# An attention and gated-layer kernel: two small matrix products written as halves of 64 columns

## The chip, the cores and the metric

The kernel runs on one NeuronCore of a Trainium2 chip. The metric is the device time of one execution in microseconds (us); lower is better. The time before is the median of three runs.

## What is computed

The reference is attention with random features, followed by a gated layer. q, k and v have 8 batches, 8 heads, 576 positions and 64 columns. With x scaled by 1 / 64^(1/4):

```
phi(x) = exp(h - max(h)) / sqrt(128),   h = x @ omega.T - sum(x*x)/2      # 128 features
kv  = phi(k).T @ v        z   = sum over positions of phi(k)
num = phi(q) @ kv         den = phi(q) @ z + 1e-6
x   = num / den           # heads side by side: 4608 x 512
out = (sigmoid(x @ w_gate) * (x @ w_val)) @ w_out     # 512 -> 1536 -> 512
```

All arrays are f32.

## The kernel before

**Attention.** Two batches make a unit u (four units), two heads a pair p (four pairs). The 2 x 576 positions of a unit are nine tiles of 128; tile 4, the middle one (`MID`), holds 64 positions of either batch b. Everything below runs for each u, p and b.

Keys (`keys`, from line 809): a projection of three matmuls per tile (`projected`, lines 774 to 776), the maximum on DVE, the exponential on ACT (line 841, tiles `kp` and, for the middle tile, `kmid`). Then comes the keys group at line 865: for each of the two heads, five products that accumulate over five tiles into `pkv`, 128 features by 66 columns (64 of v, and ones for z). The stationary operand is 128 x 128, the exponentials of a tile; the moving one is v, 128 x 66. Both are plain f32, and each product of the program leaves two matmul records and two weight loads in the profile. There are 32 keys groups of 10 products, so 640 records. ACT copies the result to `kv` (line 875).

Queries (`queries`, from line 882): projection, maximum, a subtraction on DVE (`h`, line 898), a transpose on PE (line 912, tile `pt`), the exponential on ACT (`qp`, line 917), and then line 933: query features by `kv` into `pn`, 128 x 66 for each tile and head. DVE divides by the last column (lines 944 to 950, first step `den`), PE transposes the result (line 958), ACT copies it and SP stores it to `xT` in DRAM. Query groups hold two tiles (four products, 64 such groups) or the middle tile alone (16 groups). In a middle group the 64 positions of either batch need another `kv`, so each product is already written as two of 64 columns, one for each half of the output's partitions.

**Gated layer.** While attention runs, the first part of the gated layer uses what attention has stored: chunks of `xT` are read back, split in a high and a low part on ACT and POOL (`xe`), and multiplied with the first four weight tiles (line 444, tile `gv`, 960 matmuls). Weights for the rest are converted on DVE and POOL at the same time. Behind attention come the remaining `gv` products, then the second pass (line 557, `gw`) and the output products (line 670, `po`).

**What sets the order.** The first phase has a planner of its own: `Turns`, with coroutines for each piece of work. A piece asks for an engine with a rank; `turn` also waits for free buffers; `use` books the estimated cost in ns on that engine. Whoever is ready and has the lowest rank goes next, and the instructions are written in that order. The `gv` products have the last rank (`2 * FILL`), so the planner puts them where PE would otherwise be free. Before chunk 0 has arrived, four matmuls into a bank that nobody reads (`unread`, line 780) are written behind each projection. The estimate for a keys group is `2 * (MID + 1) * 112` ns, for a query group of n products `n * 112`.

Of the kernel before, what the change touches and what calls it, by code (L numbers as in the profile page):

```python
# [20 lines left out]
P = 128  # L21
# [2 lines left out]
NP = H // 2  # L24
MID = T // 2


GROUPS = {"k": (((0, 1), (2, 3), (4,)), ((5, 6), (7, 8))), "q": (((0, 1), (2, 3)), ((4,), (5, 6), (7, 8)))}
E = D + 2
# [30 lines left out]
class Turns:  # L60
# [45 lines left out]
    def use(self, e, t, cost, lag):  # L106
        self.free[e] = t + cost
        return t + cost + lag
# [63 lines left out]
def attn_glu_kernel(ctx: ExitStack, tc, qT, kT, qn, kn, va, om, ident, w, out):  # L172
    nc = tc.nc
# [21 lines left out]
    def bank(i, name):  # L195
        return ps.tile([P, 512], F32, tag=f"bank{i}", bufs=1, name=name)
# [14 lines left out]
    use = turns.use  # L211
# [20 lines left out]
    def turn(engine, t, *shelves, rank=None):  # L232

        while True:
            t = yield engine, t, rank
            ready = t
            for s in shelves:
                place = s.next() if isinstance(s, Ring) else min(s.places, default=None)
                if place is None:
                    yield s  # L240
                    break
                ready = max(ready, place[0])
            else:
                if ready <= t:
                    return t, [s.take() for s in shelves]
            t = max(ready, turns.now)

    def after(event, t):
        while event.left:
            yield event  # L250
        return max(t, event.time)

    def act(n, pointer=False):
        return (165 if pointer else 120) + 0.833 * n

    def dve(n):
        return (n + 140) / 0.96
# [7 lines left out]
    PE_LAG, LAG, ISSUE, LANDS = 260, 100, 420, 3200  # L265
# [447 lines left out]
    def spot(pool, tag, i, shape, name, dtype=F32):  # L713
        return pool.tile(shape, dtype, tag=f"{tag}{i}", bufs=1, name=name)
# [84 lines left out]
    def source(pool, name, u, p, b, src):  # L799
        t0, t1 = span(name, b)  # L800
        n = (t1 - t0) * P
        held = ("raw", "v") if name == "k" else ("raw",)
        at, taken = yield from turn("SP", 0, *(places[h] for h in held))
        raw = spot(pool, "raw", taken[0], [P, (MID + 1) * P], f"raw{name}{u}_{p}_{b}")
        nc.sync.dma_start(out=raw[:, :n], in_=src[u, p, :, t0 * P : t1 * P])
        at = use("SP", at, ISSUE, LANDS)
        return at, raw, t0, taken

    def released(event, name, i):
        t = yield from after(event, 0)  # L810
        places[name].put(i, t)

    def keys(pool, u, p, b):
        rank = order["k", u, p, b]
        at, raw, t0, (i, vi) = yield from source(pool, "k", u, p, b, kT)
        v = spot(pool, "v", vi, [P, MID + 1, 2, E], f"v{u}_{p}_{b}")
        av = yield "SP", 0, rank + 0.5
        nc.sync.dma_start(out=v, in_=va[u, p, b])
        av = use("SP", av, ISSUE, LANDS)
        last = Event(turns, len(GROUPS["k"][b]))  # L820
        turns.start(released(last, "raw", i), rank)
        kp, held = {}, []
        every = kexp_ready[u, p, b]
        k_begun[u, p, b].set(at)

        def group(tiles):
            at_, id_, pp, hm, s, place, own = yield from projected(pool, "k", u, p, b, raw, t0, tiles, at, last)
            nt = len(tiles)
            at_ = yield "DVE", at_, None
            nb = pool.tile([P, 2, 2], F32, tag="nb", bufs=12, name=f"nb{id_}")[:, :nt]  # L830
            nc.vector.scalar_tensor_tensor(  # L831
                out=nb, in0=s, scalar=-1.0, in1=hm, op0=ALU.mult, op1=ALU.subtract
            )
            at_ = use("DVE", at_, 160, LAG)
            tag = "kmid" if tiles[0] == MID else "kp"
            at_, (k,) = yield from turn("ACT", at_, places[tag])
            x = spot(pool, tag, k, [P, 2 * nt, M], f"{tag}{id_}")
            for i, t in enumerate(tiles):
                kp[t] = x[:, 2 * i : 2 * i + 2, :]
                for h in range(2):  # L840
                    nc.scalar.activation(  # L841
                        out=kp[t][:, h, :], in_=pp[:, 2 * i + h, :], func=AF.Exp,
                        bias=nb[:, i, h : h + 1], scale=SCALE,
                    )
            at_ = use("ACT", at_, 2 * nt * act(M, True), LAG)
            if tag == "kmid":
                kmid[u, p] = kp[MID], k
            else:
                held.append((tag, k))
            banks.put(place, at_)  # L850
            pps.put(own, at_)
            every.set(at_)

        for tiles in GROUPS["k"][b]:
            turns.start(group(tiles), rank)
        at = yield from after(every, av)
        if b:
            at = yield from after(kexp_ready[u, p, 0], at)
            kp[MID], mid = kmid.pop((u, p))
            held.append(("kmid", mid))  # L860
        at, (place, k) = yield from turn("PE", at, banks, places["kv"])
        pkv = bank(place, f"pkv{u}_{p}_{b}")[:, : 2 * E].rearrange("p (h e) -> p h e", h=2)
        for h in range(2):
            for i in range(MID + 1):
                nc.tensor.matmul(  # L865
                    pkv[:, h, :], lhsT=kp[b * MID + i][:, h, :], rhs=v[:, i, h, :],
                    start=(i == 0), stop=(i == MID),
                )
        at = use("PE", at, 2 * (MID + 1) * 112, PE_LAG)
        places["v"].put(vi, at)  # L870
        for tag, i in held:
            places[tag].put(i, at)
        at = yield "ACT", at, None
        kv = spot(pool, "kv", k, [P, 2, E], f"kv{u}_{p}_{b}")
        nc.scalar.activation(out=kv, in_=pkv, func=AF.Copy)
        at = use("ACT", at, act(2 * E), LAG)
        banks.put(place, at)
        kvs[u, p, b] = kv
        kv_ready[u, p, b].set(at)
        turns.start(released(kv_users[u, p, b], "kv", k), rank)  # L880

    def queries(pool, u, p, b):
# [6 lines left out]
        def group(tiles):  # L889
            at_ = yield from after(kexp_ready[u, p, b], start)  # L890
            at_, id_, pp, hm, s, place, own = yield from projected(pool, "q", u, p, b, raw, t0, tiles, at_, last)
            nt = len(tiles)
            n = 2 * nt
# [12 lines left out]
            at_ = use("DVE", at_, 240 + dve(n * M), LAG)  # L906
# [6 lines left out]
            at_ = use("PE", at_, n * 109, PE_LAG)  # L913
            places["h"].put(hi, at_)
            at_ = yield "ACT", at_, None
            qp = spot(pool, "qp", qi, [P, 4, P], f"qp{id_}")[:, :n]
            nc.scalar.activation(out=qp, in_=pt, func=AF.Exp)  # L917
            at_ = use("ACT", at_, act(n * P), LAG)
            banks.put(place, at_)
            mid = tiles[0] == MID  # L920
            at_ = yield from after(kv_ready[u, p, b], at_)
            if mid:
                at_ = yield from after(kv_ready[u, p, 0], at_)
            at_, (place, xi) = yield from turn("PE", at_, banks, places["x"])
            pn = bank(place, f"pn{id_}")[:, : n * E].rearrange("p (i e) -> p i e", e=E)
            for i, t in enumerate(tiles):
                if t == MID:
                    mine = ((0, slice(0, P // 2)), (1, slice(P // 2, P)))
                else:
                    mine = ((b, slice(0, P)),)  # L930
                for h in range(2):
                    for bb, r in mine:
                        nc.tensor.matmul(  # L933
                            pn[r, 2 * i + h, :], lhsT=qp[:, 2 * i + h, r], rhs=kvs[u, p, bb][:, h, :],
                            start=True, stop=True,
                        )
            at_ = use("PE", at_, n * 112, PE_LAG)
            places["qp"].put(qi, at_)
            kv_users[u, p, b].set(at_)
            if mid:  # L940
# [1 line left out]
            at_ = yield "DVE", at_, None  # L942
# [10 lines left out]
            at_ = use("DVE", at_, 440 + dve(n * D), LAG)  # L953
# [9 lines left out]
            at_ = use("PE", at_, nt * 109, PE_LAG)  # L963
            places["x"].put(xi, at_)
            at_ = yield "ACT", at_, None
            xs = spot(pool, "xs", si, [P, 2 * P], f"xs{id_}")[:, : nt * P]
            nc.scalar.activation(out=xs, in_=px, func=AF.Copy)
            at_ = use("ACT", at_, act(nt * P), LAG)
            banks.put(place, at_)
            at_ = yield "SP", at_, -1  # L970
            o = u * 2 * S + tiles[0] * P
            nc.sync.dma_start(out=xT[p, :, o : o + nt * P], in_=xs)
            at_ = use("SP", at_, ISSUE, LANDS)
# [5 lines left out]
        for tiles in GROUPS["q"][b]:  # L979
            turns.start(group(tiles), rank)  # L980
# [157 lines left out]
```

## Time and profile before

| | us |
|---|---|
| median of three runs | 1275.88 (1274.79 to 1282.54) |
| the profiled execution | 1282.16 |
| its span, first to last instruction | 1280.1 |
| PE busy | 1185.1 (93%) |
| DVE busy | 891.5 (70%) |
| POOL, ACT busy | 565.7, 530.8 |
| line 865, matmul records, busy up to 560 us | 91.1 |
| line 933, matmul records, busy up to 560 us | 75.5 |

PE is TensorE's matmuls, PEld its weight loads, DVE VectorE, ACT ScalarE, POOL GpSimd, SP the engine that issues most transfers. A row of the timeline gives the start and the length of a run of like instructions, in us from the span's start. Records overlap: a matmul's record is longer than the step to the next one, so a cost is read from starts and not from the length of one record. The granted clock is the share of TensorE's full clock; its mean over the profiled execution is 0.949.

### The profile page before, as it was taken

The numbers are of one execution on the slowest core, as the hardware profiler recorded it, in microseconds if no ns is written. First come the engines' busy times: TensorE is split into PE (matmuls) and PEld (weight loads), VectorE is DVE, ScalarE is ACT, GpSimd is POOL, SyncE is SP. The second block draws the span as 40 slices with busy tenths as digits, with TensorE's granted clock in tenths as the row PEclk, the third lists the DMA queues.
The fourth block names the chain that finished last, engine by engine and source line by source line (L and its number), as shares of the span: only waits on it lengthen the run. The fifth ranks groups of instructions, "written<-read, shape, count | busy, mean of one in ns | idle before, by whom it ended". The sixth has DMA issues, their size and how long they took to land.

```text
span 1280.1 us, 24128 instructions
## 1 busy us (share of the span) xinstructions
PE 1185.1 (93%) x8936; PEld 1133.7 (89%) x8936; DVE 891.5 (70%) x1885; ACT 530.8 (41%) x1168; POOL 565.7 (44%) x591
## 2 busy tenths in 40 slices
PE   4859999899989898966999999999999799999998
PEld 4859989798978787855899999999999799999998
DVE  5885787779887988752475566655667777777665
ACT  4536464546453655423332223322234333433332
POOL 2544263525373545254176666666666411111111
PEclk7886998899989898978999999999999999999999
DMA  6636366546764665345423332333328575666653
GB/s 233 217 122 190 93 195 227 178 149 210 244 216 167 219 245 184 106 134 219 170 87 120 120 120 103 132 120 120 121 89 288 188 208 187 201 193 196 194 186 110
DMA packets 107734, 217.59 MB, mean 170 GB/s; under 512 B 10848, under 2 KB 48992, under 8 KB 105312
## 3 DMA queue, kind: packets, MB, share of 16 engines
q1 hardware_dynamic: 102288, 206.54, 48.0%
q10 hardware_dynamic: 5328, 9.51, 2.0%
q8 instruction: 70, 1.15, 0.4%
q14 instruction: 48, 0.39, 0.1%
HBM read 141.82 MB, written 74.19 MB: 169 GB/s over the span
## 4 chain that ended last, share of the span: by engine, by line
PE 75%; DVE 7%; DMA 6%; issue 6%; POOL 4%; SPq 1%; ACT 1%; DVEq 0%; POOLq 0%; ACTq 0%
PE gw L557 26%; PE po L670 20%; PE gv L444 10%; PE pkv L865 5%; PE pnq L933 4%; PE ptq L912 2%; PE ppq L774 1%; PE ppk L774 1%; PE ppk L776 1%; PE ppk L775 1%; PE ppq L775 1%; PE ppq L776 1%; DMA ye<-ye 1%; DVE nbk L831 1%; POOL xe L417 1%
## 5 line engine op out<-in xcount | busy, mean ns | idle before, releaser
L557 PE MATMUL gw<-xl,u 128*128 128x256 f32 x3024 | 363.5, 283 | 6.3 <-DVE u L537 3.7
L557 PEld LDWEIGHTS gw<-xl,u 128*128 128x128 f32 x3024 | 362.3, 190 | 7.5 <-DVE u L537 4.5
L670 PE MATMUL po<-u,yh 128*128 128x256 f32 x1512 | 272.5, 283 | 0.0
L670 PEld LDWEIGHTS po<-u,yh 128*128 128x128 f32 x1512 | 234.6, 190 | 0.0
L670 PE MATMUL po<-u,yl 128*128 128x256 f32 x756 | 214.0, 283 | 5.5 <-POOL yl L146 4.1
L444 PE MATMUL gv<-xe,wh 128*128 128x512 f32 (+1 forms) x640 | 198.8, 386 | 10.2 <-POOL xe L417 10.2
L145 ACT ACTIVATE yh<-yr 128x896 fp32r<-128x896 f32 x108 | 99.0, 948 | 166.7 <-DMA yr<-yl 56.3
L670 PEld LDWEIGHTS po<-u,yl 128*128 128x128 f32 x756 | 144.2, 191 | 6.2 <-POOL yl L146 4.3
L444 PEld LDWEIGHTS gv<-xe,wh 128*128 128x128 f32 x640 | 117.7, 195 | 29.8 <-POOL xe L417 14.0
L444 PE MATMUL gv<-xe,wl 128*128 128x512 f32 (+1 forms) x320 | 124.6, 389 | 18.2 <-ACT xe L407 18.2
L146 POOL TENSOR_TENSOR yl<-yr,yh 128x896 fp32r<-128x896 f32 x18 | 38.7, 2149 | 219.6 <-ACT yh L145 194.3
L661 DVE TENSOR_TENSOR yr<-yr 128x128 f32<-128x128 f32 x144 | 68.7, 509 | 60.7 <-DMA yr<-ye 52.2
L766 POOL TENSOR_TENSOR lok<-rawk,hik 128x256 fp32r<-128x256 f32 (+1 forms) x80 | 63.6, 800 | 105.3 <-ACT hik L763 102.3
L146 DVE TENSOR_TENSOR yl<-yr,yh 128x896 fp32r<-128x896 f32 x90 | 96.1, 1099 | 11.5 <-ACT yh L145 11.4
L537 DVE TENSOR_TENSOR u<-gw,p 128x256 f32<-128x256 f32 x144 | 60.7, 421 | 60.2 <-PE gw L557 52.1
L766 POOL TENSOR_TENSOR loq<-rawq,hiq 128x256 fp32r<-128x256 f32 (+1 forms) x80 | 56.1, 719 | 91.7 <-ACT hiq L763 90.2
L865 PE MATMUL pkv<-v,kpk 128*128 128x66 f32 x512 | 80.1, 306 | 15.5 <-ACT kpk L841 15.4
L865 PEld LDWEIGHTS pkv<-v,kpk 128*128 128x128 f32 x512 | 75.2, 221 | 16.9 <-ACT kpk L841 16.4
L444 PEld LDWEIGHTS gv<-xe,wl 128*128 128x128 f32 x320 | 62.7, 196 | 27.5 <-ACT xe L407 19.3
L841 ACT ACTIVATE kpk<-ppk,nbk 128x128 f32<-128x128 f32 x256 | 71.5, 390 | 29.1 <-DVE nbk L831 29.1
L933 PE MATMUL pnq<-kv,qpq 128*128 128x66 f32 (+1 forms) x640 | 75.5, 271 | 0.8 <-ACT qpq L917 0.8
L933 PEld LDWEIGHTS pnq<-kv,qpq 128*128 128x128 f32 (+1 forms) x640 | 71.0, 188 | 4.8 <-ACT qpq L917 1.7
(218 smaller groups left out, 2213.7 us busy)
## 6 DMA issues: line engine op xcount, KB each, us to landing
yl<-yl SPq DMA_DIRECT2D x36, 896.0 KB, 4.1
yr<-yl SPq DMA_DIRECT2D x72, 448.0 KB, 4.0
xr<-xT SPq DMA_DIRECT2D x68, 256.0 KB, 4.2
u<-w SPq DMA_DIRECT2D x14, 896.0 KB, 6.5
v<-va SPq DMA_DIRECT2D x32, 330.0 KB, 4.2
natk<-kn SPq DMA_DIRECT2D x36, 256.0 KB, 3.4
natq<-qn SPq DMA_DIRECT2D x36, 256.0 KB, 3.1
out<-o ACTq DMA_DIRECT2D x36, 256.0 KB, 2.8
```

What stands on the lines that cost most here:

```text
L145: nc.scalar.activation(out=hi, in_=x, func=AF.Copy)
L146: (lo_engine or nc.vector).tensor_tensor(out=lo, in0=x, in1=hi.bitcast(F32), op=ALU.subtract)
L444: nc.tensor.matmul(gv, lhsT=u[:, s], rhs=v, start=(m == 0), stop=(m == 3 * KC - 1))
L537: return nc.vector.tensor_tensor(out=o, in0=a, in1=b, op=ALU.add)
L557: nc.tensor.matmul(o, lhsT=u[:, k, s], rhs=v[:, kc, :], start=(first and m == 0), stop=(m == 5), skip_group_check=not first,)
L661: nc.vector.tensor_tensor(out=raw[:, o], in0=raw[:, a], in1=raw[:, b], op=op)
L670: nc.tensor.matmul(o, lhsT=u[:, i, :], rhs=v[:, k, :], start=(j + m == 0 and n in (1, 6, 5, 4)), stop=(j == NPAIR - 1 and m == 2), skip_gr ...
L766: nc.gpsimd.tensor_tensor(out=lo, in0=x, in1=hi.bitcast(F32), op=ALU.subtract)
L774: nc.tensor.matmul(o, lhsT=lo[:, c], rhs=omH, start=True, stop=False)
L841: nc.scalar.activation(out=kp[t][:, h, :], in_=pp[:, 2 * i + h, :], func=AF.Exp, bias=nb[:, i, h : h + 1], scale=SCALE,)
L865: nc.tensor.matmul(pkv[:, h, :], lhsT=kp[b * MID + i][:, h, :], rhs=v[:, i, h, :], start=(i == 0), stop=(i == MID),)
L933: nc.tensor.matmul(pn[r, 2 * i + h, :], lhsT=qp[:, 2 * i + h, r], rhs=kvs[u, p, bb][:, h, :], start=True, stop=True,)
```

## The change

Each keys product is written as two, one for features 0 to 63 and one for 64 to 127. They use the same moving operand, v, and write the lower and the upper half of the output's partitions. The query products of full tiles are written in the same way by query positions, as those of the middle tile already are. So the 10 products of a keys group are 20 of 64 columns, and the 4 of a query group 8. The planner's estimates go from 112 ns for each product to 116 for each pair of halves and 100 for each group: 1120 to 1260 for a keys group, 448 to 564 for a query group, 224 to 332 for a middle group.

```diff
+HALVES = slice(0, P // 2), slice(P // 2, P)
...
         for h in range(2):
             for i in range(MID + 1):
-                nc.tensor.matmul(
-                    pkv[:, h, :], lhsT=kp[b * MID + i][:, h, :], rhs=v[:, i, h, :],
-                    start=(i == 0), stop=(i == MID),
-                )
-        at = use("PE", at, 2 * (MID + 1) * 112, PE_LAG)
+                for r in HALVES:
+                    nc.tensor.matmul(
+                        pkv[r, h, :], lhsT=kp[b * MID + i][:, h, r], rhs=v[:, i, h, :],
+                        start=(i == 0), stop=(i == MID),
+                    )
+        at = use("PE", at, 2 * (MID + 1) * 116 + 100, PE_LAG)
...
             for i, t in enumerate(tiles):
-                if t == MID:
-                    mine = ((0, slice(0, P // 2)), (1, slice(P // 2, P)))
-                else:
-                    mine = ((b, slice(0, P)),)
                 for h in range(2):
-                    for bb, r in mine:
+                    for bb, r in zip((0, 1) if t == MID else (b, b), HALVES):
                         nc.tensor.matmul(
                             pn[r, 2 * i + h, :], lhsT=qp[:, 2 * i + h, r], rhs=kvs[u, p, bb][:, h, :],
                             start=True, stop=True,
                         )
-            at_ = use("PE", at_, n * 112, PE_LAG)
+            at_ = use("PE", at_, n * 116 + 100, PE_LAG)
```

The planner orders by its costs, so other instructions move too. In the rows below the numbers in a name are the pair and the first tile, then a running number; `x2` means that the row stands twice. On PE, the second keys group of the program stands in the same place, ahead of the same projection. Before:

```order
L865 MATMUL pkv_1_0_381<-v_1_0_113,kpk_1_0_307 128x66 x2
L865 MATMUL pkv_1_0_381<-v_1_0_113,kpk_1_2_347 128x66 x2
L865 MATMUL pkv_1_0_381<-v_1_0_113,kmidk_1_4_374 128x66
L865 MATMUL pkv_1_0_381<-v_1_0_113,kpk_1_0_307 128x66 x2
L865 MATMUL pkv_1_0_381<-v_1_0_113,kpk_1_2_347 128x66 x2
L865 MATMUL pkv_1_0_381<-v_1_0_113,kmidk_1_4_374 128x66
L774 MATMUL ppk_2_4_409<-omH,lok_2_4_231 128x256
```

And with the change:

```order
L867 MATMUL pkv_1_0_393<-v_1_0_113,kpk_1_0_307 64x66 x4
L867 MATMUL pkv_1_0_393<-v_1_0_113,kpk_1_2_346 64x66 x4
L867 MATMUL pkv_1_0_393<-v_1_0_113,kmidk_1_4_384 64x66 x2
L867 MATMUL pkv_1_0_393<-v_1_0_113,kpk_1_0_307 64x66 x4
L867 MATMUL pkv_1_0_393<-v_1_0_113,kpk_1_2_346 64x66 x4
L867 MATMUL pkv_1_0_393<-v_1_0_113,kmidk_1_4_384 64x66 x2
L775 MATMUL ppk_2_4_435<-omH,lok_2_4_231 128x256
```

Nothing moved here; each row of 128 columns became two of 64.

Later on PE, the middle group of pair 0 (`pnq_0_4`) and the query group behind it (`pnq_0_5`). Before, the middle group stood right behind the transposes, and a projection (`ppq_1_5`) stood between the two groups:

```order
L912 MATMUL ptq_0_5_1474<-id_sb,hq_0_5_1454 128x128 x4
L933 MATMUL pnq_0_4_1484<-kv_0_0_359,qpq_0_4_1472 64x66
L933 MATMUL pnq_0_4_1484<-kv_0_1_1183,qpq_0_4_1472 64x66
L933 MATMUL pnq_0_4_1484<-kv_0_0_359,qpq_0_4_1472 64x66
L933 MATMUL pnq_0_4_1484<-kv_0_1_1183,qpq_0_4_1472 64x66
L774 MATMUL ppq_1_5_1489<-omH,loq_1_5_1337 128x256
L775 MATMUL ppq_1_5_1489<-omL,hiq_1_5_1336 128x256
L776 MATMUL ppq_1_5_1489<-omH,hiq_1_5_1336 128x256
L774 MATMUL ppq_1_5_1489<-omH,loq_1_5_1337 128x256
L775 MATMUL ppq_1_5_1489<-omL,hiq_1_5_1336 128x256
L776 MATMUL ppq_1_5_1489<-omH,hiq_1_5_1336 128x256
L933 MATMUL pnq_0_5_1505<-kv_0_1_1183,qpq_0_5_1496 128x66 x4
```

With the change the projection comes first and the two groups stand side by side:

```order
L914 MATMUL ptq_0_5_1595<-id_sb,hq_0_5_1572 128x128 x4
L775 MATMUL ppq_1_5_1605<-omH,loq_1_5_1441 128x256
L776 MATMUL ppq_1_5_1605<-omL,hiq_1_5_1440 128x256
L777 MATMUL ppq_1_5_1605<-omH,hiq_1_5_1440 128x256
L775 MATMUL ppq_1_5_1605<-omH,loq_1_5_1441 128x256
L776 MATMUL ppq_1_5_1605<-omL,hiq_1_5_1440 128x256
L777 MATMUL ppq_1_5_1605<-omH,hiq_1_5_1440 128x256
L931 MATMUL pnq_0_4_1619<-kv_0_0_369,qpq_0_4_1600 64x66
L931 MATMUL pnq_0_4_1619<-kv_0_1_1265,qpq_0_4_1600 64x66
L931 MATMUL pnq_0_4_1619<-kv_0_0_369,qpq_0_4_1600 64x66
L931 MATMUL pnq_0_4_1619<-kv_0_1_1265,qpq_0_4_1600 64x66
L931 MATMUL pnq_0_5_1626<-kv_0_1_1265,qpq_0_5_1612 64x66 x8
```

The middle group moved behind the projection. In the whole order of before, halves stand in 16 stretches; with the change in 106.

## Prediction

> **What bounds the kernel now.** I read the page's totals first, then the busy time by stage, the chain of waits of the stage in which the changed products lie, and then single stretches of the timeline.
>
> ```profile
> PE 1185.1 (93%) x8936; PEld 1133.7 (89%) x8936; DVE 891.5 (70%) x1885; ACT 530.8 (41%) x1168; POOL 565.7 (44%) x591
> 0.00:110.00 110.00, 74.48 (x499) 73.24 (x500) 77.21 (x161) 55.44 (x152) 47.88 (x49) 0.79 0.58 196
> 110.00:560.00 450.00, 424.49 (x2955) 386.53 (x2954) 365.46 (x867) 232.00 (x638) 203.45 (x225) 0.94 0.56 184
> 560.00:640.00 80.00, 60.14 (x266) 49.57 (x267) 23.41 (x34) 28.39 (x42) 30.94 (x21) 0.82 0.51 181
> 640.00:1280.00 640.00, 626.00 (x5220) 624.32 (x5219) 425.45 (x826) 214.95 (x337) 283.47 (x297) 1.00 0.46 154
> ```
>
> The columns of the last four rows are the stretch, its length, busy time of PE, PEld, DVE, ACT and POOL, and the granted clock. TensorE is the busiest engine of the program, but by stage it differs. Up to 110 us PE and DVE are busy for 74 and 77 us, so neither is full. From 110 to 560 us, attention mixed with the first part of the gated layer, PE is busy for 424.5 of 450 us and DVE for 365.5 (81%). Behind 560 us no attention is left. There PE has other products, which this change doesn't touch. So only the first 560 us can give anything.
>
> ```profile
> 0.00:110.00 110.00, 21.91 (x125) 21.54 (x126) 0.79 0.58 196
> 110.00:560.00 450.00, 69.20 (x517) 69.23 (x516) 0.94 0.56 184
> 560.00:640.00 80.00, 0.00 (x0) 0.00 (x0) 0.82 0.51 181
> L933 PE MATMUL pnq<-kv,qpq 128*128 128x66 f32 x448 | 59.3, 278 | 0.8 <-ACT qpq L917 0.8
> L933 PE MATMUL pnq<-kv,qpq 128*64 128x66 f32 x128 | 7.5, 240 | 0.0
> ```
>
> The first three rows are the stages for line 865 (keys by values) alone, PE and PEld. A product of the program leaves two matmul records here (both operands are f32), so a keys group of 10 products is 20 records and the 517 records are 25.9 of the 32 groups. The last two rows are line 933 from 110 to 560 us: 448 records are 56 of the 64 query groups of 4 full products, and 128 are all 16 middle groups. Those are already written as halves (128*64): they are the price list of this change.
>
> **One step of each kind.** The rows below are PE's timeline: start, length, line, tile, shape, count. A row's length runs from its first start to its last end. The second block comes from narrow stretches around the middle group at 521.32 us: its first 2, first 4 and all 8 records.
>
> ```profile
> 518.61 0.33 PE L865 MATMUL pkv<-v,kmidk 128*128 128x66 f32 x2
> 518.77 1.06 PE L865 MATMUL pkv<-v,kpk 128*128 128x66 f32 x8
> 519.66 0.39 PE L865 MATMUL pkv<-v,kmidk 128*128 128x66 f32 x2
> 519.89 1.06 PE L865 MATMUL pkv<-v,kpk 128*128 128x66 f32 x8
> 520.78 0.28 PE L912 MATMUL ptq<-id_sb,hq 128*128 128x128 f32 x1
> ...
> 521.11 0.27 PE L912 MATMUL ptq<-id_sb,hq 128*128 128x128 f32 x1
> 521.32 0.28 PE L933 MATMUL pnq<-kv,qpq 128*64 128x66 f32 x2
> 521.32 0.34 PE L933 MATMUL pnq<-kv,qpq 128*64 128x66 f32 x4
> 521.32 0.45 PE L933 MATMUL pnq<-kv,qpq 128*64 128x66 f32 x8
> 521.70 0.38 PE L774 MATMUL ppq<-omH,loq 128*128 128x256 f32 x1
> 521.92 0.28 PE L775 MATMUL ppq<-omL,hiq 128*128 128x256 f32 x1
> ...
> 531.92 0.49 PE L912 MATMUL ptq<-id_sb,hq 128*128 128x128 f32 x3
> 532.24 1.00 PE L933 MATMUL pnq<-kv,qpq 128*128 128x66 f32 x8
> 533.05 0.36 PE L774 MATMUL ppq<-omH,loq 128*128 128x256 f32 x1
> 533.26 0.28 PE L775 MATMUL ppq<-omL,hiq 128*128 128x256 f32 x1
> ```
>
> A full pass: 20 records from 518.61 to 520.78 are 2.17 us, 0.1085 us each. A pair of half passes: 2 records end after 0.28, 4 after 0.34, 8 after 0.45 us, so a further pair costs 0.055 to 0.06 us; I take 0.058. The two halves of a pair thus run side by side, and a pair does the work of one full pass in about half its time.
>
> The halves have a price at both ends. From the last transpose ahead of a middle group to its first record pass 0.21 us (521.11 to 521.32), and behind it the first projection's successor starts 0.22 us later (521.70 to 521.92). To compare, I count from the start of the matmul ahead to the start of the second one behind, between the same neighbours. The halves take 521.92 - 521.11 = 0.81 us for 4 pairs. The full group takes 533.26 - 532.14 = 1.12 us for 8 passes; 532.14 is the start of the last of the three transposes, 531.92 + 0.49 - 0.27. The ends alone are 0.81 - 4 x 0.058 = 0.58 against 1.12 - 8 x 0.1085 = 0.25 us. So each stretch of halves costs 0.33 us more at its ends.
>
> **The change part by part.** A keys group becomes 20 pairs: 0.81 + 16 x 0.058 = 1.74 us against 1.12 + 12 x 0.1085 = 2.42. It saves 0.68 us. A query group becomes 8 pairs: 0.81 + 4 x 0.058 = 1.04 against 1.12; it saves 0.08 us, as the ends eat most of it. Middle groups stay. In the new order two stretches of halves sometimes lie side by side: 106 stretches for the 112 groups, so six pairs of ends, 2.0 us, fall away.
>
> From 110 to 560 us: 25.9 x 0.68 = 17.6, 56 x 0.08 = 4.5, and 2.0 for the ends. Part of the groups ran at the lower clock: 69.2 us of line 865 are 13 more than 25.9 x 2.17. A third of that would go too if all were clock, but some is waiting; I take 2. Together 26.1 us of PE's time. How much of it reaches the end? The chain of waits of this stage gives the lower bound.
>
> ```profile
> by line: PE gv L444 23.4%; issue 12.9%; PE pkv L865 10.5%; PE pnq L933 9.3%; PE ptq L912 5.5%; PE ppq L774 2.9%; PE ppq L775 2.5%; PE ppq L776 2.5%; PE ppk L774 2.4%; DVE nbk L831 2.2%; PE ppk L775 2.2%; PE ppk L776 2.2%; PE pxq L958 2.2%;
> DVE denq L944 <- PE pnq L933: 48.3, 60, 2.6
> DVE mxk L786 <- PE ppk L776: 12.1, 12, 2.1
> ```
>
> Line 865 has 10.5% of 450 us on the chain, 47 of its 69 us (0.68). Line 933 has 42 of its 67 us (0.63). The upper bound is PE's busy share, 424.5 of 450 us (0.94), since the matmuls of the gated layer (gv) follow wherever attention leaves room. I take 0.8, between them: 20.9 us. DVE doesn't forbid it. The two other rows are its waits in this stage (us, times, longest): 48.3 us of its idle 84.5 are spent in front of the first division step, waiting for the very products that get shorter.
>
> Up to 110 us: 6 keys and 8 query groups, 6 x 0.68 + 8 x 0.08 = 4.7 us.
>
> ```profile
> by line: PE pkv L865 18.8%; DMA natk<-kn 9.1%; PE unread L780 7.9%; DMA natq<-qn 6.3%; PE pnq L933 4.5%; DMA rawk<-kT 4.4%; PE ptq L912 3.3%; DVE ssk L729 2.9%; PE ppk L774 2.8%; PE ppk L776 2.5%; PE ppk L775 2.5%; DVE e L154 2.3%; DVE hmq
> 20.00:80.00 60.00, 41.27 (x292) 40.66 (x293) 53.45 (x101) 30.38 (x86) 34.89 (x29) 0.76 0.44 145
> ```
>
> Line 865 has nearly all of its time on that stage's chain, but from 20 to 80 us DVE is busy for 53.5 of 60 us and takes over when PE gets ahead. Between nothing and 4.7 I take 3.
>
> The sum is 20.9 + 3, 24 us. The profiled execution took 1282.16 us (span 1280.1), near the top of the three runs; it would become 1258. Against their median of 1275.88 the forecast is 1252.
>
> The estimates move rows, but little: the rows of the order that stand with the change show the first keys groups in their old place, and a middle group moved up to the query group behind it, which is one of the six pairs of ends above. Counted over the order, the last transposes of attention follow 768 of the 960 gv matmuls in both, so the stretch from 560 us on starts with the same 192 left, and I cost the moves at nothing beyond that. What hides them is the same PE that is busy for 424.5 of 450 us; if a moved row makes PE wait there, that is the second rival below.
>
> [...]
>
> **The rivals.** *First: the side-by-side running doesn't last.* The middle group is the longest stretch shown, and its two halves have different moving operands (kv of either batch), where the new halves read the same one. If a pair took as long as a full pass, 0.1085 us, nothing would be gained and 106 - 16 = 90 new stretches would pay 0.33 us: 30 us of PE's time, 24 at the end by the 0.8, so 1300. It decides from a pair step of 0.083 us, where 32 x 20 + 64 x 8 = 1152 pairs save just those 30 us. Against it stands the measured 0.055 to 0.06. [...]
>
> *Second: PE gets ahead of its fill.* The gv matmuls need rows of attention already stored and read back.
>
> ```profile
> 490.06 0.28 PE L776 MATMUL ppk<-omH,hik 128*128 128x256 f32 x1
> 494.13 0.79 PE L444 MATMUL gv<-xe,wl 128*128 128x512 f32 x1 [3.79 <-ACT xe L407]
> 496.82 1.91 PE L865 MATMUL pkv<-v,kpk 128*128 128x66 f32 x8
> 480.00:500.00 20.00, 15.65 (x77) 13.32 (x77) 19.03 (x32) 9.15 (x26) 8.96 (x6) 0.84 0.51 159
> ```
>
> Here PE stood for 3.79 us, and then 8 passes took 1.91 us in place of 1.06: the clock fell to 0.84 on the mean of this stretch. One such spell costs the wait of 3.8 us and, at 0.85 us for 8 passes, some 2 us for a group of 20. Two more of them would take 12 us, half of the gain: 1264. For it speaks that the fill depends on attention, whose other engines don't get faster; against it, that PE waits for 25.5 of 450 us in all.
>
> *Third: DVE's waits go too.* The planner put ten key products at 1.12 us where the trace has 2.17, and four query products at 0.448 where it has 0.81 (532.24 to 533.05). Its new numbers, 1.26 and 0.564, lie nearer to the 1.74 and 1.04 above, so rows on DVE stand less in front of unfinished products. At best PE's own idle 25.5 us of the stage would halve: 12 us more, 1240. Against it: PE's longest wait for DVE in this stage is small.
>
> ```profile
> PE gv L444 <- ACT xe L407: 6.7, 2, 3.8
> PE ptq L912 <- DVE hq L898: 5.2, 5, 3.1
> ```
>
> The rows are total, times and longest. DVE holds PE up for 5.2 us of 450, so there is not much to win.
>
> *Fourth: the work that is saved was never on the path,* and the time stays at 1276. The chain's 47 and 42 us speak against it.
>
> **How the numbers follow.** Forecast 0.60, pairs that don't last 0.05, fill that runs dry 0.18, DVE's waits 0.14, nothing 0.03. A measurement of this kernel tells about 1%, 12.8 us, from no change, so the bounds are 1263.1 and 1288.6. The forecast and the third rival are faster, and half of the second, which sits on the bound: 0.60 + 0.14 + 0.09 = 0.83. Within 1%: 0.09 + 0.03 = 0.12. Slower: 0.05. The forecast's own range, with 0.65 to 0.94 of 26.1 us and 1 to 5 us early, is a gain of 18 to 30, 1246 to 1258; the three runs differ by 8 us. With the second and third rival taken in, and most of what lies beyond them left out, the range is 1237 to 1267.
>
> **What would show it.** A keys group should take 1.2 to 1.3 us from its first start to its last, pairs 0.058 us apart; if it takes over 1.7 the first rival is true. Busy time of line 865's successor should fall from 91 to below 60 us over both stages. The stage that I cut at 560 us should end near 536, and everything behind it should keep its length. If PE's waits on xe in the stage grow by 10 us or its clock falls below 0.9, the second rival took its share.

## The result and the profile after

The change brought 1276.41 us to 1236.85 (medians of four runs each; 1236.42 to 1237.61 with the change). The ratio is 0.968, with a 95% interval of 0.965 to 0.972. The direction was forecast, the size wasn't: 39.6 us in place of 24, and 1236.85 lies just outside the lower end of the range, 1237.

The first fence has the page's totals after; the second has the two stages of attention and the time behind it, in the columns of before; the third the products of the keys groups alone.

```profile
PE 1138.8 (92%) x10092; PEld 1062.0 (86%) x10092; DVE 888.4 (72%) x1885; ACT 529.6 (43%) x1168; POOL 572.8 (46%) x591
```
```profile
0.00:110.00 110.00, 74.06 (x808) 67.81 (x810) 84.18 (x179) 60.60 (x171) 53.93 (x56) 0.84 0.61 208
110.00:512.10 402.10, 377.11 (x3806) 319.27 (x3802) 354.12 (x847) 225.50 (x619) 204.00 (x218) 0.98 0.60 202
512.10:1234.60 722.50, 687.63 (x5484) 674.88 (x5484) 450.07 (x861) 243.49 (x379) 314.86 (x318) 0.98 0.46 157
```
```profile
0.00:512.10 512.10, 53.82 (x1280) 45.87 (x1280) 0.95 0.60 203
```

Attention's last product on PE now ends at 512.1 us, where before it ended at 558.2. The 46 us between the two profiled executions all arise ahead of that point: behind it stood 721.9 us, and now 722.5. The granted clock of the long stage rose from 0.94 to 0.98. The keys groups are busy for 53.8 us in place of 91.1. One of them on PE's timeline, with the record ahead and the one behind:

```profile
460.93 0.40 PE L445 MATMUL gv<-xe,wh 128*128 128x512 f32 x1
461.26 0.34 PE L867 MATMUL pkv<-v,kmidk 128*64 128x66 f32 x4
461.42 0.64 PE L867 MATMUL pkv<-v,kpk 128*64 128x66 f32 x16
461.89 0.29 PE L867 MATMUL pkv<-v,kmidk 128*64 128x66 f32 x4
462.01 0.64 PE L867 MATMUL pkv<-v,kpk 128*64 128x66 f32 x16
462.57 0.50 PE L445 MATMUL gv<-xe,wh 128*128 128x512 f32 x1
```

40 half passes start within some 1.17 us (from 461.26 to the last one's end at 462.65, less 0.22 for its length). That is the 0.058 us for each pair of the forecast, and just under its 1.2 to 1.3 us for a group.

To see where 46 us went, the time up to attention's last product can be cut in three, from the records of PE and of the clock in each trace: PE idle (the time less PE's busy time); half of the busy time at the half clock (0.50 in the trace's records); and the rest, PE's work at the full clock. The second is an estimate of what the low clock costs: it takes PE's work to last twice as long there, about as a full pass does in the streams below (0.214 us against 0.111). All numbers are us. Before, the row behind it is

```profile
0.00:558.20 558.20, 498.94 (x3452) 459.77 (x3452) 440.94 (x1025) 287.05 (x789) 251.34 (x273) 0.91 0.56 186
```

| | end of attention | PE idle | lost to the low clock | work at full clock | behind |
|---|---|---|---|---|---|
| before | 558.2 | 59.3 | 38.3 | 460.6 | 721.9 |
| the change | 512.1 | 60.9 | 17.0 | 434.2 | 722.5 |

The work shrank by 26.4 us. The low clock gave back 21.3, where the forecast had taken 2. Idle time rose by 1.6. The profiled execution of before was some 6 us over its median, with a lower clock, so against the medians the clock's part is nearer 15.

### The profile page after: what moved, and what is told of

Its sections match the earlier page's. It is cut to its first block, busy times and chain, and to the rows that moved or that the text cites. A ratio compares the mean times of both kernels' runs of the same rounds, so it can differ in the third digit from the quotient of the medians.

```text
span 1234.6 us, 26447 instructions
## 1 busy us (share of the span) xinstructions
PE 1138.8 (92%) x10092; PEld 1062.0 (86%) x10092; DVE 888.4 (72%) x1885; ACT 529.6 (43%) x1168; POOL 572.8 (46%) x591
## 4 chain that ended last, share of the span: by engine, by line
PE 70%; DVE 11%; issue 6%; POOL 5%; DMA 5%; ACT 2%; SPq 1%; POOLq 0%; DVEq 0%; ACTq 0%
PE gw L558 26%; PE po L671 20%; PE gv L445 8%; PE pnq L931 3%; PE ptq L914 3%; PE pkv L867 2%; DVE mxk L787 1%; PE ppq L775 1%; PE pxq L956 1%; PE ppk L775 1%; DVE hmq L793 1%; DMA ye<-ye 1%; POOL xe L418 1%; PE ppk L777 1%; PE ppk L776 1%
## 5 line engine op out<-in xcount | busy, mean ns | idle before, releaser
L538 DVE TENSOR_TENSOR u<-gw,p 128x256 f32<-128x256 f32 x144 | 60.7, 421 | 60.2 <-PE gw L558 52.1
L767 POOL TENSOR_TENSOR loq<-rawq,hiq 128x256 fp32r<-128x256 f32 (+1 forms) x80 | 60.3, 768 | 83.1 <-ACT hiq L764 57.3
L445 PEld LDWEIGHTS gv<-xe,wl 128*128 128x128 f32 x320 | 62.1, 194 | 22.3 <-ACT xe L408 13.1
L591 POOL TENSOR_TENSOR yl<-yl,gl 128x256 f32<-128x256 f32 x36 | 36.0, 1000 | 81.1 <-issue 39.1
L588 ACT ACTIVATE gl<-gl 128x768 f32<-128x768 f32 x36 | 30.5, 846 | 90.0 <-DVE gl L538 90.0
L914 PE MATMUL ptq<-id_sb,hq 128*128 128x128 f32 x288 | 47.4, 284 | 21.9 <-DVE hq L900 19.9
L919 ACT ACTIVATE qpq<-ptq 128x512 f32<-128x512 f32 (+1 forms) x80 | 44.5, 557 | 46.8 <-PE ptq L914 46.1
```

The source lines that it names most:

```text
L445: nc.tensor.matmul(gv, lhsT=u[:, s], rhs=v, start=(m == 0), stop=(m == 3 * KC - 1))
L538: return nc.vector.tensor_tensor(out=o, in0=a, in1=b, op=ALU.add)
L767: nc.gpsimd.tensor_tensor(out=lo, in0=x, in1=hi.bitcast(F32), op=ALU.subtract)
L914: nc.tensor.transpose(out=pt[:, i, :], in_=h_sb[:, i, :], identity=id_sb)
```

## The experiments

The change has two parts, the form of the products and the planner's estimates. My first theory (A) put the extra gain on the form: the halves shorten the work and bring the clock back sooner. Its rival (B) put it on the order that the new estimates give. The first two kernels are the two parts alone; the order of instructions on every engine is that of before in the first, and that of the change in the second. Each ratio below is to runs of before made beside it; their medians lie between 1273.2 and 1274.8 us.

**Halves with the old estimates.**

```diff
-        at = use("PE", at, 2 * (MID + 1) * 116 + 100, PE_LAG)
+        at = use("PE", at, 2 * (MID + 1) * 112, PE_LAG)
...
-            at_ = use("PE", at_, n * 116 + 100, PE_LAG)
+            at_ = use("PE", at_, n * 112, PE_LAG)
```

> All products as halves, but the planner keeps its old estimates, so the order of instructions on every engine is that of before. Theory A (the halves shorten PE's work by about 26 us and, since they keep the array fuller, TensorE's clock comes back sooner after a pause; the new order is worth little): 1236 to 1245 us, and the time at the low clock up to the end of attention falls from 95.6 us to 40 to 60. Rival B (the halves give the 26 us of work alone, the new order gives the clock): 1250 to 1256 us, low clock still 80 us or more.

1244.76 us, ratio to before 0.976 (0.971 to 0.981), within theory A's range.

**Full products with the new estimates.**

```diff
-        at = use("PE", at, 2 * (MID + 1) * 112, PE_LAG)
+        at = use("PE", at, 2 * (MID + 1) * 116 + 100, PE_LAG)
...
-            at_ = use("PE", at_, n * 112, PE_LAG)
+            at_ = use("PE", at_, n * 116 + 100, PE_LAG)
```

> Full products as before, only the planner's estimates are the new ones, so the order of instructions is that of the change. Theory A: 1270 to 1280 us, no gain that can be measured. Rival B: 1256 to 1264 us with the time at the low clock up to the end of attention below 60 us.

1258.50 us, ratio 0.986 (0.981 to 0.992), within rival B's range. So neither theory holds alone. The halves give 30 us without the order, the order gives 16 without the halves, and together they give 40.

| | end of attention | PE idle | lost to the low clock | work at full clock | behind |
|---|---|---|---|---|---|
| halves, old estimates | 521.9 | 66.6 | 22.2 | 433.1 | 719.6 |
| full, new estimates | 535.4 | 50.3 | 21.2 | 463.9 | 721.6 |

The halves take 27 us of work away and the new order none. Both bring the clock up, and nearly as far each alone (to 22.2 and 21.2 us lost) as together (17.0). But the halves in the old order add 7 us of idle time, while the new order takes 9 away.

They bring it up in different ways. The next table counts, up to attention's end and behind PE's first matmul, the pauses of PE of over 2 us and the spells at the half clock in the traces' records.

| | pauses | us in all | spells at half clock | us in all |
|---|---|---|---|---|
| before | 7 | 35.1 | 9 | 95.6 |
| halves, old estimates | 7 | 33.7 | 10 | 58.0 |
| full, new estimates | 4 | 23.4 | 6 | 54.6 |
| the change | 5 | 27.2 | 7 | 47.8 |

The halves leave the pauses as they were, and a spell lasts 5.8 us on the mean in place of 10.6. The new order has fewer pauses and fewer spells, with the same full products; that the one is the cause of the other is argued from this count.

**Halves for the keys alone, and for the queries alone,** both in the order of before. Against before, the first is this, with `HALVES` defined as in the change, and nothing else:

```diff
-                nc.tensor.matmul(
-                    pkv[:, h, :], lhsT=kp[b * MID + i][:, h, :], rhs=v[:, i, h, :],
...
+                for r in HALVES:
+                    nc.tensor.matmul(
+                        pkv[r, h, :], lhsT=kp[b * MID + i][:, h, r], rhs=v[:, i, h, :],
...
```

And the second:

```diff
...
-                    for bb, r in mine:
+                    for bb, r in zip((0, 1) if t == MID else (b, b), HALVES):
```

> Only the keys products as halves, old estimates, the order of before. By the sum of the prediction, 32 x 0.68 = 22 us of work. Theory A: work and clock together, 1240 to 1250 us. Rival B: 1254 to 1258 us, low clock as before.

> Only the query products of full tiles as halves, old estimates, the order of before. By the sum of the prediction, 64 x 0.08 = 5 us of work. Theory A: 1266 to 1273 us, as query groups are short and seldom follow a pause. Rival B: 1270 to 1273 us.

The keys alone took 1260.24 us, ratio 0.987 (0.980 to 0.993); the queries alone 1268.86, ratio 0.995 (0.991 to 0.998). The work fell by 19.2 us in the first (460.6 to 441.4) and by 5.0 in the second (to 455.6), against 22 and 5 in the sum. The low clock cost 24.1 us in the first and 28.7 in the second. For the keys both ranges were missed, theory A's 1240 to 1250 and rival B's 1254 to 1258: there PE's idle time rose from 59.3 to 72.6 us. Two of its waits up to attention's end (total, times, longest), first before, then with the keys halves:

```profile
PE ptq L912 <- DVE hq L898: 17.1, 7, 7.1
PE gv L444 <- ACT xe L407: 6.7, 2, 3.8
```
```profile
PE ptq L915 <- DVE hq L901: 22.3, 10, 7.1
PE gv L446 <- ACT xe L409: 6.7, 2, 3.8
```

PE gets ahead of DVE, while its wait for the fill (`xe`) on ACT stays the same.

**Halves in turn.** The same halves and the same order as in the first experiment, but in a keys group five products of the lower half, then five of the upper, so that passes hardly ever stand beside one in the other half. The query halves still alternate.

```diff
-            for i in range(MID + 1):
-                for r in HALVES:
+            for r in HALVES:
+                for i in range(MID + 1):
```

> As the halves with old estimates, but in a keys group the five products of features 0 to 63 come first and then the five of 64 to 127, so that no product stands beside its other half. If the gain of a keys group comes from neighbours in different halves of the array running side by side, a half pass costs its own 0.055 us or more here, a group lasts some 2.2 us again and the time goes back towards 1268 us. Rival: the shorter weight load of 64 columns is what matters, a group stays near 1.2 us and the time near that of the halves with old estimates.

1253.55 us, ratio 0.985 (0.980 to 0.990): 9 us slower than alternating halves, but 20 faster than before, between the two expectations. The work is 455.0 us at the full clock, the same as with the query halves alone (455.6), so the keys halves in turn save none. But the low clock cost 14.2 us, in place of 28.7 with the query halves alone and 38.3 before. This is the form of the products acting on the clock, in the order of before and with no less work in the keys.

**Streams.** Two small programs show the step and the clock by themselves. They multiply random numbers and store zeros; attention and the gated layer are left out. Each stream is 100 full products or as many as halves, which is 200 or 400 records, followed by 100 dense matmuls. The core of the second; the first has another `gap`, without the line that reads the dense result:

```python
def gap(k):
    nc.vector.tensor_copy(out=slow[:, :256], in_=last[0])
    for _ in range(7):
        nc.vector.tensor_scalar(out=slow, in0=slow, scalar1=0.5, scalar2=0.25, op0=ALU.mult, op1=ALU.add)
...
for k, one in enumerate((full, halves, in_turn, full, halves, in_turn)):
    one(k, gap(k))
    dense(k + 1)
```

> Another program that leaves attention and the gated layer out: it multiplies random numbers and stores zeros. Twice in turn: a pause of PE of about 10 us, then 100 full products of 128 columns, a pause, the same as alternating halves, a pause, the same as halves in turn (ten lower, then ten upper), each followed by 100 dense matmuls of 128x256. [...] Rival C (the clock comes back after a fixed time of any work, and its times in the kernel were chance): equal times at the low clock in all three. Steps at the full clock: 0.1085 us for each full pass, 0.058 for each pair of alternating halves, about 0.11 for two half passes in turn.

> The program of streams again (attention and the gated layer left out, zeros stored), now with pauses that begin only when PE has finished. Theory A: after a pause of some 9 us the 200 passes of full products stay at the low clock for over 10 us, the halves for under 7. Rival C (a fixed time of any work brings the clock back): equal times at the low clock behind all pauses, 3 to 7 us.

In the first program the pauses were covered by the dense matmuls ahead of them, so only the steps can be read. Its trace has no record of the clock. That it was full is read from the dense runs: behind the first one, 100 dense matmuls took 12.23 to 12.26 us each time, as at a granted clock of 1.00 in the second program (12.26). Start, length, and count in the timeline of PE:

```profile
20.45 22.44 PE L54 MATMUL full<-v,a 128*128 128x66 f32 x200
...
54.87 11.95 PE L61 MATMUL half<-v,a 128*64 128x66 f32 x400
...
78.94 20.26 PE L70 MATMUL turn<-v,a 128*64 128x66 f32 x400
```

A full pass is 0.111 us (22.2 over 200), a pair of alternating halves 0.059 (11.7 over 200), and two half passes in turn 0.100. Side by side is what makes the halves cheap, and it lasts for 400 in a row. In the second program every stream began after a pause of 6.5 us. Its timeline, and its stretches with the columns length, busy time of PE, PEld, DVE, POOL, and clock. The last three rows are the whole spells at the half clock around the first stream of each kind:

```profile
27.16 42.94 PE L57 MATMUL full<-v,a 128*128 128x66 f32 x200 [6.54 <-DVE a L41]
69.85 13.70 PE L51 MATMUL d<-vr,wr 128*128 128x256 f32 x100
90.08 13.59 PE L64 MATMUL half<-v,a 128*64 128x66 f32 x400 [6.54 <-DVE a L41]
```
```profile
27.16:69.85 42.69, 42.69 (x201) 42.69 (x201) 0.00 (x0) 0.00 (x0) 0.50 0.00 0
90.08:103.60 13.52, 13.52 (x401) 13.45 (x401) 0.00 (x0) 0.00 (x0) 0.87 0.01 4
122.39:145.04 22.65, 22.65 (x400) 22.58 (x400) 0.00 (x0) 0.00 (x0) 0.88 0.01 2
163.84:206.53 42.69, 42.69 (x201) 42.69 (x201) 0.00 (x0) 0.00 (x0) 0.50 0.00 0
25.40:73.15 47.75, 45.99 (x215) 45.99 (x216) 1.63 (x3) 0.00 (x0) 0.50 0.00 0
86.80:93.60 6.80, 3.52 (x64) 3.52 (x66) 3.08 (x5) 0.00 (x0) 0.50 0.00 0
120.95:127.80 6.85, 5.41 (x56) 5.41 (x57) 1.35 (x2) 0.00 (x0) 0.50 0.00 0
```

After the pause the full products ran for all of their 42.7 us at half the clock, twice, with PE busy throughout. The halves were back at the full clock after about 3.5 us (13.52 us at 0.87), and so were the halves in turn after about 5.4. These two don't differ: the spell lasted some 6.8 us in both, and the streams began at different points of it. With the full products it lasted 47.8. In the second round the three streams take 42.69, 13.48 and 22.63 us, at a mean clock of 0.50, 0.87 and 0.88 again. So theory A is shown as far as the form brings the clock back sooner; the reason that it gives, a fuller array, is not shown. It doesn't explain what the estimates did.

**Larger estimates.** The next kernel was meant to show that the order is worth little. Against the change:

```diff
-        at = use("PE", at, 2 * (MID + 1) * 116 + 100, PE_LAG)
+        at = use("PE", at, 2 * (MID + 1) * 116 + 330, PE_LAG)
...
-            at_ = use("PE", at_, n * 116 + 100, PE_LAG)
+            at_ = use("PE", at_, n * 116 + 330, PE_LAG)
```

> The change with 330 ns in place of 100 for each group, which is what the ends of a stretch of halves cost in the trace of before. Theory A (order is worth little): within 4 us of the change, 1233 to 1241. Rival B (a truer order is worth much): 1225 to 1232 us.

It took 1212.50 us, ratio to before 0.952 (0.948 to 0.957). So theory A falls as far as the order goes, and rival B had asked for too little. A third theory (D) took its place: what the planner lacked was the true length of these products. The next kernels give it that length for full products, far too much for halves, and the larger number to the keys alone. The first, against before:

```diff
-        at = use("PE", at, 2 * (MID + 1) * 112, PE_LAG)
+        at = use("PE", at, 2 * (MID + 1) * 218, PE_LAG)
...
-            at_ = use("PE", at_, n * 112, PE_LAG)
+            at_ = use("PE", at_, n * (116 if tiles[0] == MID else 218) + (330 if tiles[0] == MID else 0), PE_LAG)
```

> Full products, with the estimates that the trace of before gives for them: 218 ns each, middle groups 116 a pair and 330 for the ends. Theory D (what the planner lacked was the true length of these products; with it rows stand less in front of unfinished work, whatever the form): 1225 to 1245 us, well below the 1258 of full products with the estimates of the change, and 15 to 30 us above the halves with larger estimates, since the work itself is 26 us longer. Rival E (the larger estimates help only because they are written for halves, or by chance of the order): 1250 to 1262 us.

1229.25 us, ratio 0.967 (0.960 to 0.973); rival E is out. Full products in the order that their true length gives are in the median faster than the whole change (by 7.6 us; one run of four, 1240.00, was slower), and two numbers did it.

Against the change, the next one is

```diff
-        at = use("PE", at, 2 * (MID + 1) * 116 + 100, PE_LAG)
+        at = use("PE", at, 2 * (MID + 1) * 116 + 800, PE_LAG)
...
-            at_ = use("PE", at_, n * 116 + 100, PE_LAG)
+            at_ = use("PE", at_, n * 116 + 800, PE_LAG)
```

and the one after it has `+ 330` in the first of these lines, and the second line as in the change.

> Halves, with 800 ns for each group in place of 100, well above what the groups take. Theory D (true estimates are best): 1215 to 1235 us, slower than the 1212 with 330, since the planner now leaves PE free where it is not and only 488 of the 960 gv matmuls stand ahead of attention's end. Rival F (the larger the better, because gv matmuls left for the tail fill its pauses): below 1210 us.

> Halves, the estimate of the keys groups with 330 for the ends, that of the query groups as in the change. Theory D: most of what larger estimates gain hangs on the 80 query groups, in front of whose results DVE waits, so 1228 to 1238 us here. Rival: the 32 keys groups carry half of it or more, 1215 to 1224 us.

They took 1233.43 us (ratio 0.968, 0.962 to 0.974) and 1217.60 (ratio 0.956, 0.951 to 0.961). The first puts rival F out. The second is a miss of theory D as I had put it: the keys' estimate carries most of the gain over the change (19 of 24 us), not that of the queries. Then the same two lines with `+ 200` and with `+ 450`, against the thought that each order is a draw:

> Halves with 200 ns for each group, between the 100 of the change (1236.9) and 330 (1212.5). Theory D (the nearer to the true length, the fewer rows that stand in front of unfinished work): between the two, 1219 to 1231 us. Rival H (each order is a draw, and 330 was a lucky one): anywhere from 1212 to 1245, with no trend.

> Halves with 450 ns for each group, somewhat above the true length, between 330 (1212.5) and 800 (1233.4). Theory D: a flat bottom, 1210 to 1220 us. Rival H: no trend, as far as 1235.

They took 1225.70 us (ratio 0.961, 0.957 to 0.965) and 1216.62 (ratio 0.955, 0.951 to 0.959). Together, for halves:

| added to each group | old | 100 | 200 | 330 | 450 | 800 |
|---|---|---|---|---|---|---|
| time, us | 1244.8 | 1236.9 | 1225.7 | 1212.5 | 1216.6 | 1233.4 |
| DVE's wait for pn, us | 33.5 | 20.1 | 17.4 | 10.9 | 6.3 | 0.5 |
| gv matmuls ahead of attention's end | 768 | 768 | 768 | 710 | 662 | 488 |

(The old column has 112 for each product and nothing added.) The time has its bottom near the 330 that the ends of a stretch cost in the trace; six points in order look like a curve and not like draws. Two things move with the estimate. DVE's wait in front of the division falls, as these rows show (us in total, times, longest); they are in turn full products with the old estimates (before), with the new ones and with the true ones, then halves with the old estimates, with 100, and with 330:

```profile
DVE denq L944 <- PE pnq L933: 52.1, 64, 2.6
```
```profile
DVE denq L944 <- PE pnq L933: 31.3, 49, 2.5
```
```profile
DVE denq L944 <- PE pnq L933: 6.8, 16, 1.2
```
```profile
DVE denq L942 <- PE pnq L931: 33.5, 51, 2.5
```
```profile
DVE denq L942 <- PE pnq L931: 20.1, 36, 1.4
```
```profile
DVE denq L942 <- PE pnq L931: 10.9, 21, 2.3
```

For the same form DVE waits 6.8 us in place of 52.1 once the length is right. A planner that books 1.12 us where PE needs 2.17 writes rows of the next engines before their input can be there; that they hold up what stands behind them is my reading. And with longer products the planner finds less room for gv ahead of attention's end. Up to 330 to 450 that fits: the tail had pauses in which PE waited for xe. First the change behind 512 us, then halves with 330 behind 492 us, up to 640:

```profile
PE gv L445 <- ACT xe L408: 11.9, 2, 8.1
PE gv L445 <- POOL xe L418: 7.2, 2, 5.0
```
```profile
PE gv L445 <- POOL xe L418: 7.6, 1, 7.6
PE gv L445 <- ACT xe L408: 1.2, 1, 1.2
```

10.3 us of these waits are gone, and with 58 more gv matmuls behind attention the rest of the program is no longer (721.0 us). With 800, 280 more stand behind it and the rest takes 765.2.

Neither accounts for most of the gain over the change. The kernel with the larger number for the keys alone has all 768 gv matmuls ahead of attention's end, and is 19 us faster than the change all the same. Its row for DVE's wait, and its row up to attention's end at 496.3 us:

```profile
DVE denq L942 <- PE pnq L931: 17.1, 34, 1.8
```
```profile
0.00:496.30 496.30, 445.97 (x4604) 382.45 (x4604) 434.83 (x1026) 284.81 (x789) 253.69 (x273) 0.97 0.62 210
```

DVE's wait is only 3 us less than with the change (20.1), so that row doesn't measure the gain either. What fell is PE's own idle time, 50.3 us against 60.9, and the low clock's cost, 9.8 against 17.0, with the same work (436.2 against 434.2). PE has three pauses of over 2 us there, 17.1 us in all, against the change's five and 27.2. Which of the moved rows removed them, no run shows.

**Halves for the keys, full products for the queries,** each with its true length. The keys products are written as in the change; the estimates, against before:

```diff
-        at = use("PE", at, 2 * (MID + 1) * 112, PE_LAG)
+        at = use("PE", at, 2 * (MID + 1) * 116 + 330, PE_LAG)
...
-            at_ = use("PE", at_, n * 112, PE_LAG)
+            at_ = use("PE", at_, n * 116 + 330 if tiles[0] == MID else n * 218, PE_LAG)
```

> Keys products as halves with 330 for the ends, query products of full tiles as full ones with 218 ns each. The halves of the queries were worth 64 x 0.08 = 5 us by the sum. Theory D with that sum: 1213 to 1222 us, up to 8 above the 1212.5 of all halves with 330. Rival G (with true estimates the ends of the short stretches cost more than the halves save): below 1210 us.

1211.26 us, ratio 0.950 (0.946 to 0.953), between the two ranges and the same as 1212.50 within their spreads (1209.45 to 1213.10 and 1210.08 to 1215.49). The query halves earn nothing, once the order is right. Both of these kernels beat before by 5% and the change by 2%.

## Why the prediction was wrong

- *Pairs side by side, 0.055 to 0.06 us:* right. 0.059 over 200 pairs in the streams, and a keys group as forecast. The first rival is out: 400 half passes in a row started 0.03 us apart (11.7 us over 400).
- *Work saved:* nearly right. Without the 2 us for the clock the sum has 24.1 us in the long stage and 4.7 early, 28.8; it was 26.4 up to attention's end.
- *A share of 0.8 reaching the end:* a little too high. Up to attention's end, the halves took 27.5 us of work away and added 7.3 of idle time in the order of before, a share of 0.73. In the new order (full products against halves) it is 29.7 and 10.6, or 0.64, about what the chain of waits gave. The change as a whole added only 1.6 us of idle time because the new order alone took 9.0 away, so this is not the step that failed.
- *"Some is waiting; I take 2" for the low clock:* the first step that failed. I counted only the keys groups' own loss at the low clock. Over all of PE's work it cost 38.3 us up to attention's end before and 17.0 with the change (the estimate of the tables), so the term was 21 us in the profiled executions and against the median some 15. Either part alone gives most of it: the halves in the old order 16, with shorter spells, and the new order with full products 17, with fewer pauses.
- *"I cost the moves at nothing beyond that":* the second step that failed. The new order alone brought 16 us. I had seen that the old estimates were half of the true length, and that DVE waited 48 us for these products, and put it all into a rival with at most 12 us more and a chance of 0.14. The rival's waits did fall (52.1 to 20.1 us), but it priced idle time alone, and most of what the order brought alone came by the clock (17 us, against 9 of idle time). The row that I set against it, 5.2 us in which DVE holds PE up, left out shorter waits for DVE (1.6 and 0.8 us) and all that lies ahead of 110 us. I looked at how many gv matmuls stood ahead of the end, found 768 in both, and took that for "little moved".
- *Fill that runs dry:* not as the second rival had it. PE did get ahead: the keys halves alone had 13.3 us more idle time. But its waits for `xe` rose there by only 1.4 us (9.4 to 10.8) and fell to 4.2 with the change, and the clock of the long stage rose; PE waited for DVE and POOL ahead of attention's own products (for DVE's `hq` 22.3 us with the keys halves alone and 17.1 before; for POOL's `lok` 11.6 with the change and 9.8 before).
- *Which part weighed more:* open in part. In the old order the halves are worth 30 us, in the new one 22 (1258.50 to 1236.85), and with true lengths 17 (1229.25 to 1212.50). What in the new order removes the pauses is open too.
- *The number:* the halves alone brought 30 us where the whole forecast had 24, and the order another 10 on top of them where it had nothing. The two gains overlap (30 and 16 alone, 40 together), so how much of the miss belongs to each step can't be told more closely.

## What to carry to other kernels

When a planner's costs change together with the code, build each alone before pricing either: here two numbers, set to what the trace shows, took 45 us off with the old form of the products, where the new form alone took 30. Read such costs from starts in the trace, ends included. Then change one number at a time: the longest wait pointed at the query products, and the number for the keys gave most. Where small full-width f32 products run among pauses, look at the granted clock before and after, not only at their own length.

## What the runs showed of the hardware

In the second program of streams PE was busy with full products without a break and did not get its clock back. After a pause of 6.5 us, f32 products with a 128x128 stationary and a 128x66 moving operand ran for 42.7 us at a granted clock of 0.50, 0.214 us for each pass, and the clock came up only 3.3 us into the dense matmuls behind them (73.2 us from the span's start). The same products as halves had it back after 3.5 us, and as halves in turn after 5.4, both at the end of a spell of some 6.8 us that began in the pause. With the clock up, the full products kept it: 0.111 us for each pass over two streams of 22.4 us. So in these streams a busy PE was not enough. The reason is not shown: half passes in turn have 66 moving columns each as well, and follow each other every 0.050 us where a full pass takes 0.111, but no run here varies that by itself.
